# A two-MLP memory attention kernel: the two products of the first MLP are issued under a higher scheduler priority

## The chip, the cores and the metric

The program runs on one core of a Trainium2 chip. The metric is device microseconds of one execution of the whole program. Before the change three runs gave 918.80, 922.19 and 926.05 us; their median is 922.19 us. A measurement of this kernel can tell about one per cent from no change.

The core has four engines that compute, each with an instruction queue that it works off strictly in order: PE (TensorE, matrix products), DVE (VectorE), ACT (ScalarE) and POOL (GpSimd). A fifth, SP, only starts DMA transfers here. An engine that waits at an instruction holds everything behind it in its queue.

## The reference

```python
def _attn_ref(q, k, v, phi):                      # 4 batches, 8 heads, 576 tokens, 64 wide
    a = np.exp(phi - np.max(phi, axis=2, keepdims=True))
    a = a / (np.sum(a, axis=2, keepdims=True) + 1e-09)          # over the tokens, 32 memories
    k_m = np.einsum('bhsm,bhsd->bhmd', a, k)
    v_m = np.einsum('bhsm,bhsd->bhmd', a, v)
    scores = scale * np.matmul(q, k_m.transpose(0, 1, 3, 2))
    attn = np.exp(scores - np.max(scores, axis=-1, keepdims=True))
    attn = attn / (np.sum(attn, axis=-1, keepdims=True) + 1e-09)
    return np.matmul(attn, v_m)
# first MLP: 2304 tokens, 512 -> 2048 -> 512
h = x @ w_in;  g = h / (1 + np.exp(-1.702 * h));  x = g @ w_out
# second MLP: 512 -> 1536 -> 512
xn = x / np.sqrt(np.mean(x * x, axis=-1, keepdims=True) + 1e-06) * rms_g
g = xn @ w_gate;  out = (g / (1 + np.exp(-g)) * (xn @ w_val)) @ w_out
```

q, k, v and phi come as float32. The weights of both MLPs come as float64 and have to be brought to float32 on the chip.

## The kernel before

Every float32 product is made of three passes over rounded parts (high times high, low times high, high times low), so each operand exists as a pair "h" and "l". The four batches are two pairs. attn @ v_m @ w_in is computed as attn @ (v_m @ w_in), so the first MLP starts from v_m @ w_in.

**Attention** is done in units (batch, group of four heads): pair 0 consists of the units (0,0) to (1,1), pair 1 of (2,0) to (3,1). One unit is a chain of small steps that alternate between engines: the maximum over the tokens (PE transposes L229 and L237, DVE, ACT copy L242), the subtraction (POOL L244, 96x768), the exponential (ACT L245 with a table load before it), a sum (DVE L251), the products with k and v (PE L275, tile pk, and the sums L283, tile pk4s), the division by the sums (DVE L287, L290, L291, ACT L297 and L302), transposes (PE L314 to L316), then for q transposes (L338), the scores (PE L360), their softmax (DVE L369 to L384, ACT L374, POOL L385) and the transposes of the result (PE L397, ACT L402).

**The first MLP** runs feature-major over blocks of 256 hidden units: 8 blocks (groups) for each pair, in the order pair 0, groups 0 to 7, then pair 1, groups 0 to 7. Each group has four units t (one half of a batch each). `a_g1` (L442) multiplies the attention with v_m @ w_in on PE (L454, 12 matmuls, tiles pg1 in a PSUM pool of 3), takes the gelu on ACT (L460, tile gf), the rounded part on ACT (L462, tile gr) and the rest on POOL (L109, gr). `a_g2` (L467) multiplies with w_out on PE (L483, 24 matmuls for a unit, tiles pg2 in another PSUM pool of 3) and adds each of four results into x on DVE (L491).

**Weights.** `w_load` lets SP load 128x512 float64 values (three buffers, raw). `w_conv` turns them into float32 on the bits: ACT L152 (absolute value), POOL L153 (clamp), DVE L157, L161 and L164 (shift and merge, tile cv, three buffers); then a DMA on ACT's queue stores the float32 weights for the second pair (L168), POOL L102 rounds them and POOL L109 takes the rest. A group of the first MLP needs four such pieces (two of w_in, two of w_out). On pair 1 the weights are reloaded from that store.

**Order.** The program is written as a list of steps; a scheduler then decides the order of every engine's queue, by priority, along a timeline that it simulates. The first steps are a table written by hand; units 8 to 60 of the first MLP and on (groups 2 to 7 of pair 0, most of pair 1) are written by `run`, a loop that writes for each unit: `a_g1` of this unit, a `w_conv` and a `w_load` of the next group, `vm_next` (v_m @ w_in of the next group, already under `tc.high_priority(100)`), up to two steps of side work (the attention of pair 1, later the RMS norm of pair 0), and `a_g2` of the unit before. Then a second table covers the change to the second MLP, and `run(70, ...)` the rest of it (`b_g3`, `b_g4`). Without an explicit priority, work written earlier is ahead.

Of the kernel before, what the change touches and what calls it, by code (L numbers as in the profile page):

```python
# [18 lines left out]
def kernel(  # L19
# [14 lines left out]
    """Every float32 product is taken as three float32r passes: x = h + l exactly, h being x  # L34
    rounded to float32r, and x*y = h*h' + l*h' + h*l' in float32 accumulation.

    Attention: attn @ v_m @ w_in is taken as attn @ (v_m @ w_in), per batch and head. Two batches
    (a pair) share the array when v_m @ w_in is worked out. The MLPs run feature-major over blocks
    of their hidden units (256 wide), so each weight is loaded and split once per pass; the sums
    over blocks are kept in SBUF.  # L40

    Columns of a pair: batch, parity, chunk pair, p, for token 6 p + 2 (chunk pair) + parity.
    """
# [19 lines left out]
    MINW = 2.0**-15  # bits 0x38000000  # L63
    MAXW = 122872.0  # bits 0x47EFFC00
# [47 lines left out]
    # The first MLP's float32 weights, as they are worked out on the first pass over them.  # L112
    cache = dramp.tile([NA * 4, P, 512], F32, tag="cache", name="cache")
    wt, loaded = {}, {}
# [27 lines left out]
    def w_conv(hf, clamp=G, to_h=G, to_l=G):  # L142
        """float64 to float32, on the bits: sign and top exponent bit, then the other exponent
        bits and the fraction 3 to the left. What is out of float32's range is clamped."""
# [33 lines left out]
    # A unit is four heads of a batch. Where its k and v lay, q^T and the softmax of its scores follow.  # L178
    # The four 32-row blocks of an odd batch hold heads 2, 3, 0, 1.
# [164 lines left out]
    def soft(u, hp):  # L344
        """Of a unit's softmax, blocks 2 hp and 2 hp + 1, by parity and chunk pair; and its sums."""
# [60 lines left out]
    vm = {}  # L406

    def vm_part(pr, g, c):
# [16 lines left out]
        # An odd batch's heads 2, 3, 0, 1 lie in its blocks, so the rows' halves  # L425
        # are of different batches.
# [233 lines left out]
    def vm_next(pr, g, *cs):  # L660
        with tc.high_priority(100):
            for c in cs:
                vm_part(pr, g, c)

    def narrow():
        start_up[0] = False

# [149 lines left out]
```

## Time and profile before

| | before |
|---|---|
| time, median of 3 runs (lowest, highest) | 922.19 us (918.80, 926.05) |
| profiled execution: span from first to last instruction | 919.6 us |
| PE busy, share of the span | 866.3 us, 94% |
| DVE, ACT, POOL busy | 556.7, 382.2, 496.5 us |
| mean granted clock of PE | 0.988 |

The profiled execution's time of its own is given by its span, 919.6 us; it lies inside the range of the three runs and 2.6 us below their median. A row of a timeline has the start in us, the duration, the engine ("ACTq" or "SPq" marks an instruction that only starts a DMA), the line, the operation and the tiles, output before input; in square brackets stands the idle time of the engine just before it and the instruction whose end released it. Buffer numbers are left out of the names in the profile, and pk, pq, pg are shortened names of PSUM tiles.

### The profile page before, as it was taken

The numbers are of one execution on the slowest core, as the hardware profiler recorded it, in microseconds if no ns is written. First come the engines' busy times: TensorE is split into PE (matmuls) and PEld (weight loads), VectorE is DVE, ScalarE is ACT, GpSimd is POOL, SyncE is SP. The second block draws the span as 40 slices with busy tenths as digits, with TensorE's granted clock in tenths as the row PEclk, the third lists the DMA queues.
The fourth block names the chain that finished last, engine by engine and source line by source line (L and its number), as shares of the span: only waits on it lengthen the run. The fifth ranks groups of instructions, "written<-read, shape, count | busy, mean of one in ns | idle before, by whom it ended". The sixth has DMA issues, their size and how long they took to land.

```text
span 919.6 us, 14798 instructions
## 1 busy us (share of the span) xinstructions
PE 866.3 (94%) x5702; PEld 823.1 (90%) x5702; DVE 556.7 (61%) x997; ACT 382.2 (42%) x823; POOL 496.5 (54%) x450
## 2 busy tenths in 40 slices
PE   3887997997999999999998999999999999999997
PEld 2776997986999999999988999999999999999997
DVE  5699896788965456558778155366348328333333
ACT  2366773654667765554466342122122122111110
POOL 2377998897987695979994162064046018001000
PEclk9989998999999999999999999999999999999999
DMA  9974559433221120223313021012004001000123
GB/s 215 258 218 124 165 137 244 160 118 108 90 70 46 48 69 25 69 73 101 92 47 92 1 92 46 1 46 92 0 1 124 14 1 47 1 1 1 46 58 103
DMA packets 40534, 74.62 MB, mean 81 GB/s; under 512 B 3856, under 2 KB 16144, under 8 KB 40464
## 3 DMA queue, kind: packets, MB, share of 16 engines
q1 hardware_dynamic: 35856, 65.29, 26.2%
q10 hardware_dynamic: 4608, 8.39, 2.6%
q8 instruction: 45, 0.74, 0.3%
q14 instruction: 25, 0.20, 0.1%
HBM read 60.56 MB, written 13.11 MB: 80 GB/s over the span
## 4 chain that ended last, share of the span: by engine, by line
PE 72%; POOL 8%; DVE 7%; DMA 6%; issue 4%; SPq 2%; ACT 1%; ACTq 0%; POOLq 0%; DVEq 0%
PE pg L577 31%; PE pg L608 16%; PE pg L483 14%; PE pg L454 7%; POOL cv L153 2%; DMA stage<-in_k_dram 2%; DVE cv L161 2%; PE pvm L422 2%; DMA raw_a_out<-in_moe_w_out_dram 2%; POOL gr L109 2%; DVE cv L164 1%; DVE x L491 1%; DMA stage<-in_v_dram 1%; DVE cv L157 1%; DMA raw_a_in<-in_moe_w_in_dram 1%
## 5 line engine op out<-in xcount | busy, mean ns | idle before, releaser
L483 PE MATMUL pg<-gr,a_outh 128*128 128x288 f32 x1024 | 231.4, 301 | 11.7 <-DVE x L491 10.2
L483 PEld LDWEIGHTS pg<-gr,a_outh 128*128 128x128 f32 x1024 | 172.8, 190 | 16.4 <-DVE x L491 14.7
L483 PE MATMUL pg<-gr,a_outl 128*128 128x288 f32 x512 | 151.6, 297 | 0.0
L153 POOL TENSOR_SCALAR cv<-cv 128x512 f32<-128x512 f32 x67 | 137.1, 2051 | 22.8 <-ACT cv L152 20.8
L608 PE MATMUL pg<-b_o2h,pp 128*128 128x512 f32 x432 | 139.7, 391 | 0.0
L586 DVE TENSOR_TENSOR pf<-sg,pg 128x384 f32<-128x384 f32 x72 | 39.6, 552 | 158.2 <-PE pg L577 151.0
L109 POOL TENSOR_TENSOR gr<-gf,gr 128x288 fp32r<-128x288 f32 x128 | 115.9, 920 | 34.8 <-ACT gr L462 30.1
L491 DVE TENSOR_TENSOR x<-x,pg 128x288 f32<-128x288 f32 x224 | 95.9, 446 | 61.8 <-PE pg L483 60.7
L102 POOL TENSOR_SCALAR b_o2h<-cv 128x512 fp32r<-128x512 f32 x12 | 8.4, 716 | 223.6 <-PE pg L577 223.4
L584 ACT ACTIVATE sg<-pg 128x384 f32<-128x384 f32 x72 | 35.4, 492 | 159.1 <-PE pg L577 159.0
L483 PEld LDWEIGHTS pg<-gr,a_outl 128*128 128x128 f32 x512 | 97.1, 190 | 0.0
L608 PEld LDWEIGHTS pg<-b_o2h,pp 128*128 128x128 f32 x432 | 81.1, 188 | 16.1
L588 ACT CAST pp<-pf 128x384 fp32r<-128x384 f32 x72 | 37.0, 513 | 126.9 <-DVE pf L586 126.6
L608 PE MATMUL pg<-b_o2l,pp 128*128 128x512 f32 x216 | 84.8, 393 | 0.0
L616 DVE TENSOR_TENSOR oacc<-oacc,pg 128x512 f32<-128x512 f32 x90 | 61.1, 683 | 24.1 <-PE pg L608 24.1
L460 ACT ACTIVATE gf<-pg 128x288 f32<-128x288 f32 x128 | 51.6, 410 | 53.4 <-POOL gr L109 25.2
L109 DVE TENSOR_TENSOR pp<-pf,pp 128x384 fp32r<-128x384 f32 x72 | 46.3, 643 | 34.9 <-ACT pp L588 34.9
L462 ACT CAST gr<-gf 128x288 fp32r<-128x288 f32 x128 | 53.5, 432 | 28.8 <-PE pg L483 25.3
L577 PE MATMUL pg<-xnh,b_gateh 128*128 128x384 f32 x288 | 62.6, 337 | 0.0
L577 PE MATMUL pg<-xnh,b_vall 128*128 128x384 f32 x288 | 62.3, 337 | 0.0
L577 PE MATMUL pg<-xnh,b_gatel 128*128 128x384 f32 x288 | 62.3, 336 | 0.0
L157 DVE TENSOR_SCALAR cv<-cv 128x512 uint32<-128x512 uint32 x68 | 52.0, 765 | 17.0 <-POOL cv L153 16.9
(183 smaller groups left out, 1849.4 us busy)
## 6 DMA issues: line engine op xcount, KB each, us to landing
raw_a_in<-in_moe_w_in_dram SPq DMA_DIRECT2D x16, 512.0 KB, 4.2
raw_a_out<-in_moe_w_out_dram SPq DMA_DIRECT2D x16, 512.0 KB, 4.3
cache<-cv ACTq DMA_DIRECT2D x32, 256.0 KB, 3.8
raw_b_gate<-in_moe_w_gate_dram SPq DMA_DIRECT2D x12, 512.0 KB, 3.7
raw_b_val<-in_moe_w_val_dram SPq DMA_DIRECT2D x12, 512.0 KB, 3.8
raw_b_o<-in_moe_w_out_dram SPq DMA_DIRECT2D x12, 512.0 KB, 3.6
stage<-in_k_dram SPq DMA_DIRECT2D x8, 576.0 KB, 12.1
stage<-in_v_dram SPq DMA_DIRECT2D x8, 576.0 KB, 11.6
```

The source lines that it names most:

```text
L109: eng.tensor_tensor(out=lo, in0=full, in1=hi.bitcast(F32), op=ALU.subtract)
L153: clamp.tensor_scalar(out=t.bitcast(F32), in0=t.bitcast(F32), scalar1=MINW, scalar2=MAXW, op0=ALU.max, op1=ALU.min,)
L157: nc.vector.tensor_scalar(out=t, in0=t, scalar1=3, scalar2=0x3FFFFFFF, op0=ALU.logical_shift_left, op1=ALU.bitwise_and,)
L454: nc.tensor.matmul(ps[:, :HALF], lhsT=a[:, b, c, f], rhs=at[:, y, c, n], start=(i == 0), stop=(i == 5),)
L460: nc.scalar.activation(out=gf[:, :HALF], in_=ps[:, :HALF], func=AF.Gelu_apprx_sigmoid)
L462: nc.scalar.copy(out=gr[:, 0, :HALF], in_=gf[:, :HALF])
L483: nc.tensor.matmul(ps[:, :HALF], lhsT=wo[a][:, fc, es], rhs=gr[fc][:, y, :HALF], start=(i == 0), stop=(i == 5),)
L491: nc.vector.tensor_tensor(out=acc[:, e, n], in0=acc[:, e, n], in1=ps[:, :HALF], op=ALU.add)
L577: nc.tensor.matmul(ps[:, :TB], lhsT=w[a][:, e, f], rhs=xs[y][:, e, n], start=(i == 0), stop=(i == 3 * NE - 1),)
L586: nc.vector.tensor_tensor(out=pf, in0=sg, in1=pss[1][:, :TB], op=ALU.mult)
L608: nc.tensor.matmul(ps, lhsT=pp[fc][:, a, ks], rhs=w[y][:, fc], start=(i == 0), stop=(i == 5))
L616: nc.vector.tensor_tensor(out=o, in0=o, in1=ps, op=ALU.add)
```

## The change

A helper `first(n)` opens the scheduler's `high_priority(n)` for n above 0, and does nothing for 0. Inside `run`, the calls of `a_g1` and of `a_g2` are put under `first(150)`; those of `b_g3` and `b_g4` under `first(0)`. The side work, `w_conv` and `w_load` keep their priority, `vm_next` its 100. No instruction is added, removed or altered. Comments and docstrings are dropped too, and the lines of `run` move down by up to five.

```diff
+    def first(n):
+        return tc.high_priority(n) if n else nullcontext()
+
...
         for j, (i, key, t) in list(enumerate(units))[lo:hi]:
             if key == ("a", 1, 0) and t == 1:
                 side, per = norm_side(0), 1
-            (a_g1 if key[0] == "a" else b_g3)(*key[1:], t)
+            with first(150 if key[0] == "a" else 0):
+                (a_g1 if key[0] == "a" else b_g3)(*key[1:], t)
             for hf in at_slot.get(j, []):
                 w_conv(hf)
                 done += 1
...
             for s in islice(side, per):
                 do(s)
-            (a_g2 if prev[0] == "a" else b_g4)(*prev[1:])
+            with first(150 if prev[0] == "a" else 0):
+                (a_g2 if prev[0] == "a" else b_g4)(*prev[1:])
             prev = (*key, t)
```

The effect is on the order of the queues, between the end of the first table (about 112 us into the span) and about 410 us; before and after that stretch PE's order is the same in both kernels. Three places are shown. Numbers behind a tile's name are the program's, the same in both kernels.

ACT's queue in group 4 of pair 0. cache is the store of converted weights, pg_1858 a result of `a_g1`; in brackets are the semaphores that a row waits for, and DMAHW with a number is one of the eight semaphores that the DMAs share. Before:

```order
L152 ACTIVATE cv<-raw_a_4_out_1804 128x512 [waits DMAHW6_49,DMAHW5_49,Pool_49]
L168 DMA cache<-cv 128x512 [waits DMAHW0_49,DVE_49]
L460 ACTIVATE gf<-pg_1769 128x288 [waits PE_49,Pool_49]
L460 ACTIVATE gf<-pg_1781 128x288 [waits PE_49,Pool_49]
L462 CAST gr<-gf 128x288 [waits PE_49,Activation_49]
L242 COPY kmisc_1_1440<-pk_1616 96x128 [waits PE_49]
L168 DMA cache<-cv 128x512 [waits DMAHW2_49,DVE_49]
L462 CAST gr<-gf 128x288 [waits PE_49,Activation_49] x2
L168 DMA cache<-cv 128x512 [waits DMAHW5_49,DVE_49]
L460 ACTIVATE gf<-pg_1858 128x288 [waits Pool_49]
L462 CAST gr<-gf 128x288 [waits PE_49,Activation_49]
L245 ACT_TABLE_LOAD [waits DMAHW7_49]
```

The change:

```order
L152 ACTIVATE cv<-raw_a_4_out_1804 128x512 [waits DMAHW6_49,DMAHW5_49,Pool_49]
L460 ACTIVATE gf<-pg_1769 128x288 [waits PE_49,Pool_49]
L460 ACTIVATE gf<-pg_1781 128x288 [waits PE_49,Pool_49]
L168 DMA cache<-cv 128x512 [waits DMAHW2_49,DVE_49]
L462 CAST gr<-gf 128x288 [waits PE_49,Activation_49] x2
L152 ACTIVATE cv<-raw_a_4_out_1891 128x512 [waits DMAHW3_49,Pool_49]
L168 DMA cache<-cv 128x512 [waits DMAHW4_49,DVE_49]
L462 CAST gr<-gf 128x288 [waits PE_49,Activation_49]
L460 ACTIVATE gf<-pg_1858 128x288 [waits Pool_49]
L242 COPY kmisc_1_1440<-pk_1616 96x128
L460 ACTIVATE gf<-pg_1870 128x288 [waits Pool_49]
L462 CAST gr<-gf 128x288 [waits PE_49,Activation_49] x2
```

Two stores stand between the gelus of pg_1781 and pg_1858 in both. The last of them waited for DMAHW5, which the k load of unit (3,1) uses; now it waits for DMAHW4, which the k load of unit (3,0) uses, three loads earlier on SP's queue, and L152 of raw_a_4_out_1891 stands ahead of it. Four rows behind the fence's end another store waits for DMAHW6 (the q load of unit (3,0)). The load of raw_a_4_out_1891 moves on SP's queue from behind the six loads of the units (3,0) and (3,1) to ahead of them.

DVE's queue in group 6 of pair 0, where the last w_out piece of the group is converted (L157, L161, L164 with raw_a_6_out_2627). Before:

```order
L491 TENSOR_TENSOR x_0_822<-x_0_822,pg_2562 128x288 [waits PE_49]
L491 TENSOR_TENSOR x_0_822<-x_0_822,pg_2570 128x288 [waits PE_49]
L491 TENSOR_TENSOR x_0_822<-x_0_822,pg_2578 128x288 [waits PE_49]
L157 TENSOR_SCALAR cv<-cv 128x512 [waits DMAHW2_49,Pool_49]
L161 SCALAR_TENSOR_TENSOR cv<-raw_a_6_out_2627,cv 128x512 [waits DMAHW3_49,DVE_49]
L164 SCALAR_TENSOR_TENSOR cv<-raw_a_6_out_2627,cv 128x512 [waits DVE_49]
L491 TENSOR_TENSOR x_0_822<-x_0_822,pg_2586 128x288 [waits PE_49]
L491 TENSOR_TENSOR x_0_822<-x_0_822,pg_2643 128x288 [waits PE_49]
L491 TENSOR_TENSOR x_0_822<-x_0_822,pg_2651 128x288 [waits PE_49]
```

The change:

```order
L491 TENSOR_TENSOR x_0_822<-x_0_822,pg_2578 128x288 [waits PE_49]
L384 RECIPROCAL stage_1_1443<-stage_1_1443 96x12 [waits DVE_49]
L491 TENSOR_TENSOR x_0_822<-x_0_822,pg_2586 128x288 [waits PE_49]
L157 TENSOR_SCALAR cv<-cv 128x512 [waits DMAHW2_49,Pool_49]
L161 SCALAR_TENSOR_TENSOR cv<-raw_a_6_out_2627,cv 128x512 [waits DMAHW3_49,DVE_49]
L491 TENSOR_TENSOR x_0_822<-x_0_822,pg_2643 128x288 [waits PE_49]
L164 SCALAR_TENSOR_TENSOR cv<-raw_a_6_out_2627,cv 128x512 [waits DVE_49]
L157 TENSOR_SCALAR cv<-cv 128x512 [waits DMAHW5_49,Pool_49]
L491 TENSOR_TENSOR x_0_822<-x_0_822,pg_2651 128x288 [waits PE_49]
L161 SCALAR_TENSOR_TENSOR cv<-raw_a_7_in_2710,cv 128x512 [waits DMAHW4_49,DVE_49]
L491 TENSOR_TENSOR x_0_822<-x_0_822,pg_2659 128x288 [waits PE_49]
```

The adds L491 stood in one block ahead of the three steps of the conversion and one behind; now one add stands between each two of the steps. On POOL, the subtraction L244 of unit (3,0) stood right behind the clamp of this piece; now it comes in the next group, behind a low part of `a_g1`.

PE's queue at the end of pair 0, where unit (3,1), the last unit of attention, is worked out. pk_3074 is its product with k and v, pk4s its sums, pk_3112 the transposes of the divided result, pq_3189 and pq_3194 transposes of q. Before:

```order
L483 MATMUL pg_3315<-gr,a_6_outl 128x288
L275 MATMUL pk_3074<-stage_1_2826,kmisc_1_2823 32x128 x24
L283 MATMUL pk4s<-ones_f,kmisc_1_2823 128x1
L483 MATMUL pg_3315<-gr,a_6_outh 128x288 x2
L483 MATMUL pg_3315<-gr,a_6_outl 128x288
L483 MATMUL pg_3315<-gr,a_6_outh 128x288
L483 MATMUL pg_3359<-gr,a_7_outh 128x288
L483 MATMUL pg_3359<-gr,a_7_outl 128x288
L483 MATMUL pg_3359<-gr,a_7_outh 128x288 x2
L483 MATMUL pg_3359<-gr,a_7_outl 128x288
L483 MATMUL pg_3359<-gr,a_7_outh 128x288
L483 MATMUL pg_3367<-gr,a_7_outh 128x288
```

The change:

```order
L483 MATMUL pg_3545<-gr,a_7_outh 128x288
L275 MATMUL pk_3074<-stage_1_2826,kmisc_1_2823 32x128 x24
L283 MATMUL pk4s<-ones_f,kmisc_1_2823 128x1
L314 MATMUL pk_3112<-ident,kz 128x128
L315 MATMUL pk_3112<-ident,kz 128x128
L316 MATMUL pk_3112<-ident,vz 128x128
L338 MATMUL pq_3189<-ident,stage_1_2826 128x96 x3
L338 MATMUL pq_3194<-ident,stage_1_2826 128x96 x3
L422 MATMUL pvm<-a_0_inh,vlh_1006 128x256
L454 MATMUL pg_3493<-attnT_536,vm_7h 128x288 x2
L454 MATMUL pg_3493<-attnT_536,vm_7l 128x288 x2
L454 MATMUL pg_3493<-attnT_536,vm_7h 128x288 x2
```

Before, 30 matmuls of L483 and L454 lay between the sums pk4s and the transposes pk_3112 (the fence shows the first half of them). Now pk_3112 follows the sums at once, then pq_3189, and what lay between (the work on pg_3359 to pg_3383) is ahead of pk_2900, the first step of the same unit. From pk_2971 (L237) to the first transposes of the unit's result (L397), PE has 204 matmuls of L483, L454 and L422 in its queue before, and 140 now.

## Rows read from the trace of the kernel before

**Rows 1.** The page, parts 1 and 2: busy time of the engines, and busy tenths in 40 slices of 23 us each.

```profile
PE 866.3 (94%) x5702; PEld 823.1 (90%) x5702; DVE 556.7 (61%) x997; ACT 382.2 (42%) x823; POOL 496.5 (54%) x450
...
PE   3887997997999999999998999999999999999997
...
POOL 2377998897987695979994162064046018001000
PEclk9989998999999999999999999999999999999999
```

**Rows 2.** Busy time by stretch: start and end in us, length, busy time and instructions of PE, PEld, DVE, ACT, POOL, granted clock, DMA share, GB/s.

```profile
120.00:260.00 140.00, 124.43 (x988) 119.27 (x987) 116.85 (x218) 79.71 (x176) 125.45 (x110) 0.96 0.52 145
260.00:310.00 50.00, 50.00 (x435) 49.64 (x435) 25.38 (x56) 36.62 (x83) 38.61 (x43) 1.00 0.20 54
310.00:410.00 100.00, 100.00 (x768) 99.98 (x768) 60.30 (x125) 60.23 (x140) 77.14 (x86) 1.00 0.19 55
```

**Rows 3.** What PE waited for between 120 and 260 us: us in total, times, longest us.

```profile
PE pg L483 <- DVE x L491: 9.5, 8, 5.2
PE pg L454 <- ACT gf L460: 4.0, 1, 4.0
PE pq L397 <- POOL stage L385: 1.1, 1, 1.1
```

**Rows 4.** Timelines of ACT, PE and SP around 157 us.

```profile
156.68 0.33 ACTq L168 DMA_DIRECT2D cache<-cv  x1
157.06 0.41 ACT L460 ACTIVATE gf<-pg 128x288 f32<-128x288 f32 x1 [7.65 <-DMA stage<-in_k_dram]
...
163.52 0.68 ACT L152 ACTIVATE cv<-raw_a_out 128x512 f32<-128x512 f32 x1 [0.48 <-DMA raw_a_out<-in_moe_w_out_dram]
...
153.18 0.29 PE L483 MATMUL pg<-gr,a_outh 128*128 128x288 f32 x1
157.52 0.85 PE L454 MATMUL pg<-attnT,vm_3h 128*128 128x288 f32 x2 [4.04 <-ACT gf L460]
...
136.41 2.39 SPq L209 DMA_DIRECT2D stage<-in_k_dram  x1
```

**Rows 5.** The chain of waits between 130 and 166 us: start, us, what.

```profile
136.41 20.20 DMA stage<-in_k_dram
```

**Rows 6.** Timelines of DVE, POOL and PE around 215 us, and one row of PE at 129 us.

```profile
213.12 0.73 DVE L157 TENSOR_SCALAR cv<-cv 128x512 uint32<-128x512 uint32 x1
213.88 5.53 DVE L161 SCALAR_TENSOR_TENSOR cv<-raw_a_out,cv 128x512 uint32<-128x512 uint32 x1
219.44 1.16 DVE L164 SCALAR_TENSOR_TENSOR cv<-raw_a_out,cv 128x512 uint32<-128x512 uint32 x1
...
213.54 2.02 POOL L244 TENSOR_TENSOR kmisc<-kmisc 96x768 f32<-96x768 f32 x1
215.51 0.79 POOL L109 TENSOR_TENSOR gr<-gf,gr 128x288 fp32r<-128x288 f32 x1
216.28 0.61 POOL L102 TENSOR_SCALAR a_outh<-cv 128x512 fp32r<-128x512 f32 x1
216.86 0.79 POOL L109 TENSOR_TENSOR gr<-gf,gr 128x288 fp32r<-128x288 f32 x1
217.61 1.26 POOL L109 TENSOR_TENSOR a_inl<-cv,a_inh 128x512 fp32r<-128x512 f32 x1
218.82 1.24 POOL L109 TENSOR_TENSOR gr<-gf,gr 128x288 fp32r<-128x288 f32 x1
...
221.03 0.58 PE L483 MATMUL pg<-gr,a_outh 128*128 128x288 f32 x1 [5.25 <-DVE x L491]
...
129.50 0.40 PE L483 MATMUL pg<-gr,a_outh 128*128 128x288 f32 x1 [1.34 <-DVE x L491]
```

**Rows 7.** Busy time by stretch behind the two longest idle times of PE, columns as in rows 2.

```profile
157.50:161.00 3.50, 3.48 (x14) 3.48 (x15) 0.88 (x1) 3.45 (x4) 0.80 (x1) 0.50 1.06 244
161.00:164.00 3.00, 3.00 (x54) 2.44 (x53) 0.98 (x2) 2.45 (x6) 1.65 (x2) 0.66 1.03 384
...
221.00:225.00 4.00, 3.97 (x52) 3.58 (x56) 2.15 (x4) 3.95 (x5) 1.55 (x2) 0.57 0.64 197
```

**Rows 8.** The instructions of L161 between 120 and 260 us: ns min/median/max, first and last start.

```profile
L161 DVE SCALAR_TENSOR_TENSOR cv<-raw_a_out,cv x10: 675/706/5527, 123.4 to 250.5; 128x512 uint32<-128x512 uint32 x10
```

**Rows 9.** Timelines of PE, ACT and DVE between 261 and 295 us, rows of unit (3,1) alone.

```profile
261.94 0.27 PE L237 MATMUL pk<-ident,mx 128*96 128x128 f32 x1
...
265.67 0.85 ACT L245 ACTIVATE kmisc<-kmisc 96x768 f32<-96x768 f32 x1
...
268.37 0.54 PE L275 MATMUL pk<-stage,kmisc 96*32 96x128 f32 x12
...
269.82 0.38 PE L283 MATMUL pk4s<-ones_f,kmisc 96*128 96x1 f32 x2
...
270.63 0.97 DVE L291 TENSOR_SCALAR rv<-maskeo,rv 128x3 f32<-128x3 f32 x1
...
272.58 0.31 ACT L297 ACTIVATE kz<-pk,rv 128x64 f32<-128x64 f32 x1
...
274.10 0.27 PE L314 MATMUL pk<-ident,kz 128*128 128x128 f32 x1
...
294.20 0.49 PE L397 MATMUL pq<-ident,stage 96*128 96x96 f32 x4
```

**Rows 10.** Busy time by stretch at the same place, columns as in rows 2.

```profile
262.20:268.37 6.17, 6.17 (x49) 6.01 (x47) 3.18 (x5) 5.52 (x9) 4.83 (x6) 1.00 0.16 41
...
262.20:294.20 32.00, 32.00 (x295) 31.64 (x294) 19.32 (x44) 22.48 (x48) 23.51 (x27) 1.00 0.15 42
```

More of the change, by code (lines that the diff above doesn't have):

```diff
@@ L1 @@
-from contextlib import ExitStack
+from contextlib import ExitStack, nullcontext
 from itertools import islice
```

## The prediction

> **What bounds the kernel now.** I read the page first: PE is busy 94% of the span, so only its idle time and its slow clock can be won, and both lie before 260 us and once near 485 us [rows 1]. The table by stretch says it in numbers: from 260 to 410 us PE is busy 150.0 of 150.0 us at clock 1.00, and from 120 to 260 us it lacks 15.6 of 140 us at clock 0.96 [rows 2]. In the first of these two, a new order can only lose; in the second it can win. From 410 us PE's order is the same in both kernels, so I carry whatever is won or lost by then to the end unchanged.
>
> What PE waits for between 120 and 260 us is almost all the MLP's own evacuations, not weights and not PE: 9.5 us for the adds L491 in eight waits, one of them 5.2, and one wait of 4.0 us for the gelu L460 [rows 3]. Both long ones are side work ahead of the MLP in a queue:
>
> - At 157 us ACT sits 7.65 us in front of a gelu. The instruction ahead of it is a store of converted weights, which starts at 156.68; the chain of waits shows why: it waits for a k load of attention, issued at 136.41 and landed 20.20 us later, at 156.61 [rows 4, 5]. The store has nothing to do with that load but the semaphore. PE is idle 4.04 us for it [rows 4].
> - At 213.88 a step of the weight conversion, L161, takes 5.53 us on DVE, where its median is 0.71 [rows 6, 8]. During it POOL runs L244 and five more instructions without a gap [rows 6]. One add stands behind L161 and L164 on DVE, and PE is idle 5.25 us [rows 6].
>
> **What the change does, part by part.** No instruction is added or removed; what moves is the order of PE, ACT, DVE, POOL and SP. The sum is made against the profiled execution, 919.6 us; the median of the runs is 2.6 us higher.
>
> *The store at 157 us.* In the new order the store ahead of this gelu waits for the k load of unit (3,0), three loads earlier, while the w_out load, moved ahead, comes in front. From 156.61 the v and q loads of (3,1) and the w_out load land by 163.52 [rows 4, 5], so a load takes about 6.9 / 3 = 2.3 us. The k load of (3,0) then lands near 156.6 − 3 × 2.3 + 2.3 = 152.0, and the next store's load, q of (3,0), near 156.6. PE had work until 153.5 [rows 4], so the gelu at 152 is in time. Gone is the idle 4.0 us. Gone too is the slow clock behind it: 3.5 us at 0.50 (the lower of its two levels, 1.2 of 2.4 GHz) and 3.0 us at 0.66 [rows 7], which is 3.5 × 0.50 + 3.0 × 0.34 = 2.8 us. Together −6.8 us. The least is 0 (another store, another load), and that is an end of the range.
>
> *The conversion at 214 us.* L244 moves away from this L161 and an add comes between any two steps. Whether the next L161 meets POOL's dense stretch again is not to be read from an order, so I bound it: at best idle and clock go, 5.25 + 4.0 × 0.43 = 7.0 us [rows 6, 7]; at worst nothing. I take −5.7 us: a shorter wait for an add stays in its place, 1.3 us as at 129.50 [rows 6] (the other seven are 0.6 on average, (9.5 − 5.2) / 7 [rows 3]), and the clock stays up. The trace has L161 held for 5.53 us, over six POOL instructions [rows 6]. The Trainium skill (SBUF — State Buffer, "Who interferes with whom") says that a DVE instruction with two inputs in SBUF contends with a GpSimd instruction that reads SBUF, and that whoever has the shared pair keeps it for the whole instruction, the other being blocked. By that rule L161 would wait for L244 alone, until 215.56, and take 2.4 us; the trace disagrees with it in the length. By the rule this term would be −7.0 and the forecast 917.8, since no meeting with POOL could then hold the adds for long. By the row it is −5.7, and the row speaks against the change: low parts put ahead on POOL make such a stretch without a gap likelier.
>
> *The remaining small waits* before 260 us, 15.6 − 4.0 − 5.25 = 6.3 us [rows 2, 4, 6], I leave as they are: the adds go ahead of side work now (bound −3), but PE also gets to the next group's weights earlier, and POOL, which makes them, is busy 125.5 of 140 us [rows 2] with no priority for `w_conv`. For that I add +1 us (0 to +4).
>
> *The end of pair 0, 262 to 294 us.* This is where the displaced work falls due. Unit (3,1)'s chain runs from L237 at 261.94 to L397 at 294.20, 32.3 us, and PE is fully busy meanwhile [rows 9, 10]. In the new order PE has 64 large matmuls fewer in between (140 against 204). One costs 6.17 / 49 = 0.126 us [rows 10], so 8.1 us of cover go. Walking the chain with the new queue:
>
> 1. From L237 to the end of the exponential took 266.52 − 261.94 = 4.6 us [rows 9]; the cover is 24 matmuls, 3.1 us. Idle 1.5.
> 2. The sums end at 270.20 and the transposes L314 follow at once. Ahead of them must come the division: L291 ends at 271.60, one ACT step of 0.31 follows, so 271.95 at the earliest, 274.10 as it was [rows 9]. Idle 1.8 to 3.9; I take 2.2, since ACT is less crowded there.
> 3. The rest (the first v_m @ w_in product waits for the unit's last copies, the scores for q's transposes, L397 for the softmax) has the other 116 of the 140 matmuls and small products as cover. I put it at 1.0 for each of the three, 3.0 together, by the wait of 1.1 us for L385 [rows 3].
>
> That is 6.7 us, between 3 (ACT and DVE free at once) and 8.1 (the chain as long as before). An idle time of 5.25 us lowered the clock by 1.7 us worth [rows 6, 7]; I add it once: +8.4 us. The upper end, 8.1 and two such clock losses, is +11.5; the lower is +3.
>
> *The rest of the stretch to 410 us* (side work moved among itself, the RMS norm of pair 0): PE is saturated there [rows 2], and I cost it at nothing. Its cover is that full PE; if an L385 came late there, it would cost 1 us as in the wait for L385 [rows 3].
>
> **Sum:** −6.8 − 5.7 + 1.0 + 8.4 = −3.1 us against the profiled execution, 916.5. On the scale of the median, 922.2 − 3.1 = **919.1 us**.
>
> **Rivals.**
>
> - *Nearly all early idle time goes and the boundary is covered* (faster). For it: both long waits are the MLP behind side work, just what a priority reorders [rows 3]. Against: the sums followed at once by the transposes that need them cannot be covered. It gives −6.8 − 7.0 − 3 + 3 = −13.8: about 908. Chance 0.22, with what lies between it and my forecast.
> - *The boundary costs it all and the early stalls only move* (slower). The place is PE's queue from L237 to L397 of unit (3,1): with the attention put behind the MLP in every queue, its links wait also on ACT and POOL for gelus and low parts, so the chain stays at 32.3 us or grows with 8.1 us less on PE. It decides when the early gain is below the boundary's loss by 9 us. With +11.5 there, +1, and no early gain, 922.2 + 12.5 = 934.7. For it: POOL has no time to spare in groups 3 to 7 [rows 1, 2], so a stall of 5 us can be formed anew. Against: the first stall's reason is a plain queue order that is gone. Chance 0.22.
> - *It does nothing that shows*: what is won before 260 us is paid back at 262 to 294, as in my sum, or the order changes among waits of the same size. 913.0 to 931.4; its likeliest part is 914 to 927. Chance 0.56, my forecast within it.
>
> **How the numbers follow.** About one per cent is what a measurement of this kernel can tell from no change: below 913.0 is faster, above 931.4 slower. The likeliest is the sum, 919.1, with its own range 914 to 927 (early gain −6.8 to −13.8, boundary +3 to +11.5, not all at their ends). To hold 8 in 10 I go to the fast rival, 907, and up to 934, short of the slow rival's end. Faster 0.22, same 0.56, slower 0.22.
>
> **What the changed profile would show.** For the store: no idle time on ACT with a stage load as its releaser near 150 us, and no clock below 0.9 between 150 and 165. For the conversion: no L161 above 3 us in front of an add for which PE waits over 2 us. For the boundary: PE idle 5 to 9 us between about 245 and 285 us, released by ACT L245 and L297 and by POOL L385, with a granted clock below 1.00 behind it. For the end: from 410 us on the same intervals as before, the idle time of 3 us near 485 among them. The forecast is wrong if PE's idle time at the boundary is under 3 us, if a new wait over 3 us stands in groups 3 to 6, or if the stretch behind 410 us changes in length by over 2 us.

## The result: slower, 935.6 us

| | before, in the same comparison | the change |
|---|---|---|
| median (lowest to highest) | 920.5 us (917.5 to 926.1) | 935.6 us (934.3 to 936.8) |
| ratio, 95% interval | | 1.0149 [1.0112, 1.0186] |
| span of the profiled execution | 919.6 us | 933.8 us |

The forecast of 919.1 us and its range to 934 are missed; the time is near that of the slow rival, 934.7 us. In a second comparison the changed kernel took 931.0 us, 1.0094 [1.0064, 1.0124], so the loss is 0.9 to 1.5%, and two comparisons of one kernel can differ by half a per cent. Executions that lasted 1691 us or more are left out of the ratios, and the profiled one of h2_late_unit (2152.64 us) is among them, so that this run has a time and no rows.

The page of the changed kernel, the lines that answer to [rows 1]:

```profile
PE 871.5 (93%) x5702; PEld 824.8 (88%) x5702; DVE 563.1 (60%) x997; ACT 381.5 (41%) x823; POOL 496.5 (53%) x450
...
PE   3787988998998899999998999999999999999998
...
POOL 2377999799846686889986073045027008001000
PEclk9969999999998999999998999999999999999999
```

Busy time by stretch, as in [rows 2]:

```profile
120.00:260.00 140.00, 127.15 (x995) 120.64 (x994) 118.13 (x210) 73.96 (x169) 128.60 (x113) 0.98 0.52 148
260.00:310.00 50.00, 43.54 (x362) 41.91 (x362) 26.11 (x60) 32.11 (x67) 26.70 (x29) 0.93 0.11 32
310.00:410.00 100.00, 97.16 (x737) 95.91 (x736) 56.14 (x113) 62.39 (x143) 76.82 (x84) 1.00 0.18 54
```

From 120 to 260 us PE gained 2.7 us of busy time. From 260 to 410 us, where it had been busy without a gap, it lost 6.5 and 2.8 us, and in the first of the two stretches its clock fell to 0.93. The order of PE's matmuls is the same again not from 410 us, as I had read it, but from 430.9 us before and 444.2 in the change. From there on the two kernels run nearly alike: PE's wait for L528 near the end of the first MLP is 3.36 us before and 3.37 now, and it comes 13.4 us later (485.60 and 498.97). Around it the clock is 0.50 for longer in the change (498.1 to 504.9 us, against 487.3 to 490.7 before), and at the end the change is 14.2 us late. PE's rows before and in the change:

```profile
485.60 0.52 PE L535 MATMUL pnr<-ident,r 128*128 128x128 f32 x3 [3.36 <-DVE r L528]
```

```profile
498.97 0.87 PE L535 MATMUL pnr<-ident,r 128*128 128x128 f32 x3 [3.37 <-DVE r L528]
```

**The early part.** The stall of ACT at 157 us is gone. ACT's timeline of the changed kernel has the store at 152.19 and the gelu 0.8 us behind it, and no row there waits for a load of attention:

```profile
146.65 0.37 ACTq L168 DMA_DIRECT2D cache<-cv  x1
...
152.19 0.37 ACTq L168 DMA_DIRECT2D cache<-cv  x1
152.66 0.43 ACT L462 CAST gr<-gf 128x288 fp32r<-128x288 f32 x1 [2.29 <-DVE x L491]
153.00 0.41 ACT L460 ACTIVATE gf<-pg 128x288 f32<-128x288 f32 x1
```

The L161 of 5.53 us at 214 us is gone too, but in this execution another L161 met a like stretch of POOL, which begins with an L244 and has no gap. Timelines of DVE, POOL and PE, changed kernel:

```profile
157.85 4.21 DVE L161 SCALAR_TENSOR_TENSOR cv<-raw_a_out,cv 128x512 uint32<-128x512 uint32 x1
161.99 0.44 DVE L491 TENSOR_TENSOR x<-x,pg 128x288 f32<-128x288 f32 x1
...
157.50 2.02 POOL L244 TENSOR_TENSOR kmisc<-kmisc 96x768 f32<-96x768 f32 x1
159.48 0.81 POOL L109 TENSOR_TENSOR gr<-gf,gr 128x288 fp32r<-128x288 f32 x1
160.25 1.27 POOL L109 TENSOR_TENSOR a_outl<-cv,a_outh 128x512 fp32r<-128x512 f32 x1
161.47 1.25 POOL L109 TENSOR_TENSOR gr<-gf,gr 128x288 fp32r<-128x288 f32 x1
...
162.48 0.40 PE L483 MATMUL pg<-gr,a_outh 128*128 128x288 f32 x1 [1.85 <-DVE x L491]
```

Between 120 and 260 us PE now has 13 waits, the longest of 1.85 us; before it had 11, with the two long ones. What PE waited for there, as in [rows 3], the three largest:

```profile
PE pg L483 <- DVE x L491: 8.7, 8, 1.8
PE pg L454 <- DVE vm_3l L109: 1.3, 1, 1.3
PE pvm L422 <- ACT gf L460: 1.1, 1, 1.1
```

**The end of pair 0.** The same view between 260 and 412 us, where [rows 2] had no wait at all:

```profile
PE pg L454 <- ACT gf L460: 3.0, 4, 1.1
PE pk L314 <- ACT kz L297: 2.6, 1, 2.6
PE pg L483 <- ACT x L106: 2.3, 1, 2.3
PE pq L338 <- ACT stage L106: 0.5, 1, 0.5
```

The wait of 2.6 us is the link that follows the sums at once. The chain of waits of the changed kernel there (start, us, what):

```profile
277.86 1.40 DVE kmisc L251
...
279.31 0.40 PE pk4s L283 x2
...
279.73 0.68 DVE vm_0l L109
...
280.43 0.77 DVE vm_0l L109 x2
...
281.21 0.17 DVE rv L287
...
281.92 0.32 ACT kz L297
...
282.29 0.33 PE pk L314
```

Three DVE instructions of `vm_next` stand ahead of the division and take 1.45 us of it. The wait of 2.3 us comes later, in pair 1. ACT's and PE's timelines of the changed kernel:

```profile
301.21 1.28 ACT L374 ACT_TABLE_LOAD   x1
302.50 0.52 ACT L374 ACTIVATE stage<-stage 96x384 f32<-96x384 f32 x1
302.93 0.50 ACT L512 CAST sr<-sq 128x384 fp32r<-128x384 f32 x1
303.34 1.22 ACT L433 CAST vm_1h<-pvm 64x512 fp32r<-64x512 f32 x3
304.58 0.70 ACT L106 COPY x<-pg 128x288 f32<-128x288 f32 x2
...
305.04 0.40 PE L483 MATMUL pg<-gr,a_outh 128*128 128x288 f32 x1 [2.25 <-ACT x L106]
```

ACT is still at the softmax of unit (3,1), with a table load, while PE already needs ACT's copies of pair 1's first results. Before, the same L397 came at 294.20 [rows 9]; here it comes at 308.30.

The waits for gelus have one thing in common. When ACT changes from an exponential or from the RMS norm (L525) back to the gelu, it loads a table, 1.28 us here. ACT and PE of the changed kernel:

```profile
311.79 1.28 ACT L460 ACT_TABLE_LOAD   x1
313.08 0.71 ACT L460 ACTIVATE gf<-pg 128x288 f32<-128x288 f32 x2
...
313.54 0.54 PE L454 MATMUL pg<-attnT,vm_0h 128*128 128x288 f32 x2 [1.11 <-ACT gf L460]
```

The other waits for a gelu in this stretch stand 1.8 us behind the start of such a load as well (loads at 297.76, 316.02, 355.61 and 393.00). Before, the same stretch has five such loads (266.54 to 381.48), and PE, busy all the time, waits behind none of them.

### The profile page after: what moved, and what is told of

Its sections match the earlier page's. It is cut to its first block, busy times and chain, and to the rows that moved or that the text cites. A ratio compares the mean times of both kernels' runs of the same rounds, so it can differ in the third digit from the quotient of the medians.

```text
span 933.8 us, 14790 instructions
## 1 busy us (share of the span) xinstructions
PE 871.5 (93%) x5702; PEld 824.8 (88%) x5702; DVE 563.1 (60%) x997; ACT 381.5 (41%) x823; POOL 496.5 (53%) x450
## 4 chain that ended last, share of the span: by engine, by line
PE 68%; POOL 9%; DVE 8%; issue 5%; ACT 4%; DMA 4%; SPq 2%; ACTq 0%; POOLq 0%; DVEq 0%
PE pg L577 30%; PE pg L608 15%; PE pg L483 12%; PE pg L454 7%; POOL gr L109 3%; POOL cv L153 2%; DVE cv L161 2%; DMA raw_a_out<-in_moe_w_out_dram 2%; PE pvm L422 1%; DVE cv L164 1%; DMA stage<-in_v_dram 1%; DVE cv L157 1%; DVE x L491 1%; POOL a_inl L109 1%; POOL a_outl L109 1%
## 5 line engine op out<-in xcount | busy, mean ns | idle before, releaser
L483 PE MATMUL pg<-gr,a_outh 128*128 128x288 f32 x1024 | 231.5, 301 | 13.1 <-DVE x L491 9.8
L483 PEld LDWEIGHTS pg<-gr,a_outh 128*128 128x128 f32 x1024 | 173.1, 190 | 17.9 <-DVE x L491 13.3
L483 PE MATMUL pg<-gr,a_outl 128*128 128x288 f32 x512 | 151.2, 297 | 0.0
L491 DVE TENSOR_TENSOR x<-x,pg 128x288 f32<-128x288 f32 x224 | 96.2, 447 | 54.2 <-PE pg L483 53.3
L102 POOL TENSOR_SCALAR b_o2h<-cv 128x512 fp32r<-128x512 f32 x12 | 8.4, 715 | 224.9 <-PE pg L577 224.7
L483 PEld LDWEIGHTS pg<-gr,a_outl 128*128 128x128 f32 x512 | 97.3, 190 | 0.0
L608 PEld LDWEIGHTS pg<-b_o2h,pp 128*128 128x128 f32 x432 | 81.1, 188 | 16.1
L157 DVE TENSOR_SCALAR cv<-cv 128x512 uint32<-128x512 uint32 x68 | 55.0, 809 | 20.0 <-POOL cv L153 19.8
L577 PE MATMUL pg<-xnh,b_valh 128*128 128x384 f32 x288 | 62.4, 337 | 0.0
```

What stands on the lines that cost most here:

```text
L157: nc.vector.tensor_scalar(out=t, in0=t, scalar1=3, scalar2=0x3FFFFFFF, op0=ALU.logical_shift_left, op1=ALU.bitwise_and,)
L483: nc.tensor.matmul(ps[:, :HALF], lhsT=wo[a][:, fc, es], rhs=gr[fc][:, y, :HALF], start=(i == 0), stop=(i == 5),)
L491: nc.vector.tensor_tensor(out=acc[:, e, n], in0=acc[:, e, n], in1=ps[:, :HALF], op=ALU.add)
L577: nc.tensor.matmul(ps[:, :TB], lhsT=w[a][:, e, f], rhs=xs[y][:, e, n], start=(i == 0), stop=(i == 3 * NE - 1),)
L608: nc.tensor.matmul(ps, lhsT=pp[fc][:, a, ks], rhs=w[y][:, fc], start=(i == 0), stop=(i == 5))
```

## The experiments

I give for each run the place of the last attention unit in PE's queue: how many large matmuls (L454, L483, L422) stand ahead of its last transposes, L397 of unit (3,1). It is 1296 before and 1334 in the change. For profiled executions I sum PE's idle time and its slow clock ((1 − granted clock) × busy time) over windows of 2 us, for 112 to 260 us and for 260 to 412 us. All ratios are to the kernel before in the same comparison. Group numbers are those of pair 0; units with j below 24 are groups 2 to 5.

### Where the priority stands

```diff
-            with first(150 if key[0] == "a" else 0):
+            with first(150 if j < 24 else 0):
...
-            with first(150 if prev[0] == "a" else 0):
+            with first(150 if j < 24 else 0):
```

**e1_early.** 

> The priority of 150 ends with group 5 of pair 0; groups 6 and 7 and all of pair 1 have none, as in the kernel before. PE's order is that of the change up to group 5, and in it the first step of the last attention unit, L237 of unit (3,1), stands behind 1200 large matmuls (L454, L483, L422), against 1092 before and 1194 in the change; between that step and L397 lie 126 of them, against 204 and 140. Theory 1 (the loss is made early, by putting the attention behind the MLP, and only falls due at the end of pair 0): as slow as the change, 930 to 936 us against 920.5. Theory 2 (the loss is made by the order of group 7 and of pair 1 itself, where the MLP goes ahead of the unit's steps): the gain of groups 2 to 5 alone, 915 to 919 us.

Measured: 935.0 us, 1.0117 [1.0070, 1.0163]. Its profiled execution took 927.2 us, the other three 934.3 to 935.8, so its rows show less than its time.

```diff
-            with first(150 if key[0] == "a" else 0):
+            with first(150 if j >= 24 and key[0] == "a" else 0):
...
-            with first(150 if prev[0] == "a" else 0):
+            with first(150 if j >= 24 and prev[0] == "a" else 0):
```

**e2_late.** 

> The opposite: no priority up to group 5 of pair 0, 150 from group 6 on and in pair 1. L237 of unit (3,1) stands behind 1110 large matmuls, with 221 of them up to L397. Theory 1: like the kernel before, 919 to 924 us. Theory 2: like the change, 930 to 936 us.

Measured: 938.2 us, 1.0167 [1.0139, 1.0194].

```diff
-            with first(150 if prev[0] == "a" else 0):
+            with first(0):
```

**e4_g1.** 

> Only a_g1 has the priority of 150, a_g2 none. L237 of unit (3,1) stands behind 1073 large matmuls, with 172 of them up to L397: 32 less cover than before, 4 us at 0.126 us each, and they fall only on the places where PE has nothing else. Theory 1: 918 to 924 us. Theory 2 (the raised MLP itself): between the kernels, 924 to 932 us.

Measured: 1.0015 [0.9998, 1.0031], 923.5 us.

```diff
-            for s in islice(side, per):
-                do(s)
+            with first(150 if j < 36 else 0):
+                for s in islice(side, per):
+                    do(s)
```

**e9_side.** 

> As the change, and the attention of pair 1 has the same 150 in groups 2 to 7 of pair 0 and at the start of pair 1, so that only the weight conversion and loads stay behind. L237 of unit (3,1) stands behind 1110 large matmuls, with 216 up to L397. Theory 1: the loss at the end of pair 0 is gone, PE idle under 2 us between 260 and 330 us, and the time is 915 to 921 us. Theory 3 (the weights, put behind everything, are what is late): 930 us or more, with PE or ACT waiting for L164, L102 or raw loads.

Measured: 932.3 us, 1.0106 [1.0073, 1.0138].

Theories 1, 2 and 3 fall. The early half and the late half each cost as much as the whole, and e2_late and e9_side have 221 and 216 large matmuls between L237 and L397, more than the 204 of before, and still lose. Theory 3's time came in e9_side, but not its waits: between 112 and 412 us PE waits nowhere for L164, L102 or a raw load, and ACT once, 0.7 us, for a raw load. What the four slow kernels share is a late L397 (1326 to 1334); the fast one has an early one (1245). This suggests theory 4, which the next runs test: PE has by then worked off what doesn't need the unit, and the unit's end, with the gelus, exponentials and copies that ACT owes at the start of pair 1, lies bare.

### The place of the last unit, alone

Three runs start from the kernel before, with nothing of the MLP raised (both `first` get 0), and lower the side steps of unit (3,1) by 150, 100 and 120:

```diff
             for s in islice(side, per):
-                do(s)
+                with first(-150 if s[0].__name__.startswith("att") and (3, 1) in s else 0):
+                    do(s)
```

**h2_late_unit.** 

> The kernel before, without any priority of the MLP; only the side steps of unit (3,1) are lowered by 150. PE's order up to that unit is that of before, and its last transposes, L397, stand behind 1346 large matmuls (L454, L483, L422) instead of 1296; the change has 1334 there, and the three slow kernels run so far 1326 to 1331, the fast ones 1296 and 1245. Theory 4 (what costs is that the end of the last attention unit comes when PE has worked off nearly every matmul that does not need it, whatever put it there): as slow as the change, 930 to 938 us. Theory 5 (what costs is a_g2 put at once behind a_g1, so that PE waits for each gelu and cast): like before, 919 to 925 us.

Measured: 935.6 us (935.1 to 937.6), 1.0160 [1.0135, 1.0184].

**k100_late_unit.** 

> The kernel before with the side steps of unit (3,1) lowered by 100 instead of 150, nothing else. In PE's order L397 of that unit then stands behind 1292 large matmuls, near the 1296 of before, so that 42 of the 1334 that do not need the unit are left for its end. Theory 4: like before, 919 to 924 us. If lowering the unit's steps costs by itself, on ACT or DVE: 926 us or more.

Measured: 922.9 us, 1.0006 [0.9982, 1.0029].

**k120_late_unit.** 

> The same, lowered by 120: L397 stands behind 1346 large matmuls, L237, L275 and L314 stay behind 1092, 1142 and 1176 (1092, 1140 and 1170 before). Theory 4: 930 to 938 us, with 8 us or more of idle time and slow clock of PE between 260 and 412 us (none before, 12.5 in the change), released by ACT L460, L374's line or copies of ACT. If the place of L397 is not what counts: 919 to 925 us.

Measured: 931.5 us, 1.0100 [1.0067, 1.0134]. What PE waited for between 260 and 412 us, first k100, then k120:

```profile
PE pg L454 <- ACT gf L460: 0.4, 1, 0.4
```

```profile
PE pg L454 <- ACT gf L460: 3.8, 3, 1.8
PE pg L454 <- ACT attnT L402: 1.3, 1, 1.3
```

This is the experiment that carries the verdict. Nothing is raised, PE's order up to the unit is that of before, and the two kernels differ by 20 in one offset: with L397 behind 1292 matmuls it costs nothing, behind 1346 it costs 1%. So a late last unit is enough for a loss of this size. (That L397 can stand behind 1346 also shows that more than the 1334 of the expectations don't need the unit.) Of the 8 us expected between 260 and 412 us only 5.1 show as idle time, but the time is there: from PE's 1795th matmul to its 3111th, the same two and the same work between them in all three kernels, it takes 166.1 us before, 167.1 with 100 and 174.3 with 120. The waits agree with those of the changed kernel in part. The three for gelus stand behind a table load, as there; the one for attnT does not occur there, and the change's waits for kz and for copies into x, 4.9 us, do not occur here. The longest, 1.84 us at 349.08, comes 47 us behind L397 and behind the RMS norm's table loads; how the unit's place brings that one about is not shown.

### One product alone

```diff
-            with first(150 if key[0] == "a" else 0):
+            with first(0):
```

**e5_g2** (a_g2 raised, a_g1 not). 

> Only a_g2 has the priority of 150, a_g1 none. L397 of unit (3,1) stands behind 1331 large matmuls. Theories 4 and 5 both: as slow as the change, 930 to 938 us. If it is like before, neither holds and it takes both products together.

Measured: 926.2 us, 1.0060 [1.0038, 1.0083], slower than before, but less than both theories had. The end costs as expected, 10.4 us between 260 and 412 us, but the early part gains 10.7 (9.1 us of loss against 19.8).

```diff
-            with first(150 if key[0] == "a" else 0):
+            with first(150 if j >= 32 and key[0] == "a" else 0):
...
-            with first(150 if prev[0] == "a" else 0):
+            with first(150 if j >= 32 and prev[0] == "a" else 0):
```

**e8_pair1** (both raised in pair 1 alone). 

> The priority of 150 for both products in pair 1 alone, none in pair 0. L397 of unit (3,1) stands behind 1304 large matmuls, 8 more than before, while a_g2 goes ahead of the RMS norm and the rest of the side work in pair 1. Theory 4: like before, 919 to 925 us. Theory 5: slower, 928 us or more, with PE idle for L460 and L106 between 285 and 400 us.

Measured: 929.5 us, 1.0085 [1.0057, 1.0112]; between 260 and 412 us it loses 4.1 us, one wait of 1.96 us for a gelu and the slow clock behind it among them. The time is theory 5's, and L397 is near its old place: a raised MLP in pair 1 does cost something of its own. ACT and PE show what:

```profile
286.81 1.28 ACT L374 ACT_TABLE_LOAD   x1
...
289.10 1.28 ACT L460 ACT_TABLE_LOAD   x1
...
291.29 1.28 ACT L374 ACT_TABLE_LOAD   x1
...
293.12 1.28 ACT L460 ACT_TABLE_LOAD   x1
...
294.88 0.40 PE L454 MATMUL pg<-attnT,vm_0h 128*128 128x288 f32 x1 [1.96 <-ACT gf L460]
```

A gelu stands between the two exponentials (L374) of unit (3,1) and brings two more table loads, and PE waits for the gelu behind the last. Before, one load (283.52) serves both exponentials. The change has the same split, with loads of L374 at 295.60 and 301.21. How much of its loss is due to that is not separated; e1_early, with nothing raised in pair 1 and no split, loses as much without it.

```diff
-            with first(150 if prev[0] == "a" else 0):
+            with first(0):
...
-    run(8, 61, ("a", 0, 1, 3), side, 2)
+    run(8, 61, ("a", 0, 1, 3), side, 3)
```

**g1_g1per3** (a_g1 raised; the loop takes three side steps). 

> Only a_g1 has the priority of 150, and the loop writes three side steps for each unit where it wrote two. L397 of unit (3,1) stands behind 1243 large matmuls, so that 91 are left for its end. Theory 4: no loss at the end of pair 0, PE idle under 2 us between 260 and 330 us, and not slower than before: 916 to 923 us. Theory 5: the same, as a_g2 is not raised.

Measured: 923.1 us, 1.0011 [0.9991, 1.0030]; 1.6 us lost at the end of pair 0, as expected.

### Raised early, with the unit in its place

Of i5_g2_16; i8_g2_20_p3 has `j < 20` there, and 3 side steps as in g1_g1per3:

```diff
-            with first(150 if key[0] == "a" else 0):
+            with first(0):
...
-            with first(150 if prev[0] == "a" else 0):
+            with first(150 if j < 16 else 0):
```

**i5_g2_16.** 

> Only a_g2 has the priority of 150, and only in groups 2 and 3 of pair 0. L397 of unit (3,1) stands behind 1296 large matmuls, as before. Theory 4: nothing lost at the end of pair 0; of the early gain (10.7 us between 112 and 260 us with a_g2 raised alone all through) the part of these groups, about half: 914 to 921 us. If a raised a_g2 costs by itself: 924 us or more.

Measured: 917.6 us, 0.9945 [0.9927, 0.9963]. This version beats both kernels, by little: the gain over before is as large as the difference between the two comparisons of the changed kernel. Busy time by stretch:

```profile
112.00:260.00 148.00, 137.00 (x1100) 132.05 (x1099) 120.54 (x234) 87.23 (x192) 140.17 (x122) 0.98 0.49 140
260.00:412.00 152.00, 152.00 (x1215) 151.57 (x1214) 88.80 (x186) 97.30 (x224) 117.36 (x127) 1.00 0.20 58
```

**i8_g2_20_p3.** 

> Only a_g2 has the priority of 150, in groups 2 to 4 of pair 0, and the loop writes three side steps for each unit where it wrote two, so that the attention is written earlier. L397 stands behind 1296 large matmuls. Theory 4: nothing lost at the end of pair 0 and most of the early gain of 10.7 us kept: 911 to 918 us. If a raised a_g2 costs by itself: 924 us or more.

Measured: 921.3 us, 0.9980 [0.9965, 0.9995], above the 911 to 918 expected: nothing lost at the end, but less gained early. A raised a_g2 does not cost by itself here.

### How little is enough

The edits are those of e1_early with `j < 16` and `j < 12`, of e1_early's first line alone with `j < 16` (the second `first` gets 0), and none.

**l1_both16** (both, groups 2 and 3). 

> Both products have the priority of 150, but only in groups 2 and 3 of pair 0. L397 of unit (3,1) stands behind 1331 large matmuls, so 3 of the 1334 are left for its end. Theory 4: slower than before by the loss at the end of pair 0 (8 to 12 us) less the early gain: 925 to 935 us. If the priority must stand near the end of pair 0 to cost anything: 915 to 921 us.

Measured: 935.2 us, 1.0148 [1.0112, 1.0185].

**l3_both12** (both, group 2 alone). 

> Both products have the priority of 150 in group 2 of pair 0 alone, four units of 61. L397 of unit (3,1) stands behind 1331 large matmuls. Theory 4: 925 to 935 us, with 8 us or more of idle time and slow clock between 260 and 412 us. If so short a stretch can't cost: 919 to 923 us.

Measured: 934.4 us, 1.0128 [1.0099, 1.0158].

**l2_g1_16** (a_g1 alone, groups 2 and 3). 

> Only a_g1 has the priority of 150, in groups 2 and 3 of pair 0. L397 of unit (3,1) stands behind 1296 large matmuls, as before and as in the run with a_g2 alone in these groups (917.6 us against 922.8). Theory 4: nothing lost at the end of pair 0. If raising a_g1 removes the early waits as a_g2 does: 915 to 919 us; if the early gain is a_g2's: 920 to 924 us.

Measured: 920.5 us, 0.9986 [0.9967, 1.0006]: nothing lost at the end, no gain beyond the interval.

**after_again.** 

> The changed kernel once more, for a second profile. If its small early gain (3.7 us of idle time and slow clock less than before, between 112 and 260 us) is the kernel's own: idle time there 12 to 13.5 us and slow clock 2 to 4 us again. If it was that execution's: slow clock under 1 us there, as in the run whose priority ends with group 5 and whose order up to there is the same.

Measured: 931.0 us, 1.0094 [1.0064, 1.0124]; between 112 and 260 us 11.3 us idle and no slow clock. Neither expectation fits whole. The slow clock was the first execution's, and so was 1.5 us of the idle time: the wait of 1.85 us behind the L161 of 4.21 us has no match here. The 11.3 us agree with e1_early, whose order up to there is the same (11.5).

| run | ratio | matmuls ahead of L397 | lost 112 to 260 us (idle + slow clock) | lost 260 to 412 us |
|---|---|---|---|---|
| before | 1 | 1296 | 15.6 + 4.2 | 0 |
| g1_g1per3 | 1.0011 | 1243 | 13.2 + 3.2 | 1.6 |
| e4_g1 | 1.0015 | 1245 | 13.7 + 1.5 | 2.4 |
| k100_late_unit | 1.0006 | 1292 | 13.7 + 6.2 | 0.5 |
| i5_g2_16 | 0.9945 | 1296 | 11.0 + 2.8 | 0 |
| i8_g2_20_p3 | 0.9980 | 1296 | 14.4 + 1.6 | 0 |
| l2_g1_16 | 0.9986 | 1296 | 13.8 + 4.4 | 0 |
| e8_pair1 | 1.0085 | 1304 | 14.5 + 5.0 | 4.1 |
| e1_early | 1.0117 | 1326 | 11.5 + 0 | 11.5 |
| e9_side | 1.0106 | 1326 | 14.7 + 1.7 | 8.0 |
| e2_late | 1.0167 | 1331 | 15.7 + 3.9 | 8.9 |
| e5_g2 | 1.0060 | 1331 | 9.1 + 0 | 10.4 |
| l1_both16 | 1.0148 | 1331 | 12.5 + 1.5 | 10.4 |
| l3_both12 | 1.0128 | 1331 | 14.4 + 6.2 | 7.7 |
| the change | 1.0149 | 1334 | 12.8 + 3.3 | 12.5 |
| after_again | 1.0094 | 1334 | 11.3 + 0 | 13.9 |
| k120_late_unit | 1.0100 | 1346 | 14.7 + 4.5 | 5.1 |

Up to 1296 at most 2.4 us are lost at the end of pair 0, at 1304 4.1, and from 1326 on 5 to 14 us. Within that last group the loss does not rise with the place: the latest, k120_late_unit, shows the least.

## Why the prediction was wrong

- **The store at 157 us, −6.8 us:** right in mechanism, the wait is gone. The slow clock behind it did not go with it: in the profiled execution it was 0.66 from 154 to 158 us, after other waits. In the second execution there was none.
- **The conversion at 214 us, −5.7 us:** the L161 there is short now, at most 1.19 us from 213 us on; but the race with POOL came up again, twice: L161 took 4.21 us at 157.85, and L164, the step behind it, 2.81 us at 221.21. PE waited 1.85 and 1.52 us for the adds behind them, 3.4 where I had left 1.3. The second execution has the L164 alone. I had bounded this from an order that can't tell it.
- **The remaining small waits, +1.0 us:** with both stalls gone, 15.6 − 4.0 − 5.25 + 1.3 + 1.0 = 8.6 us of idle time should have been left; 12.8 were (11.3 the second time). Without the waits behind L161 and L164 that is about +3 us for this term, inside its 0 to +4.
- **The early part as a whole** was −11.5 us; it measured −3.7 (19.8 to 16.1), and −8.5 in the second execution. Two steps failed here: that the clock stays up once the stalls are gone (3.3 us of slow clock in the first execution, none in the second), and the size of the waits that are left (4.2 us too many, 2.7 the second time). Raising a_g2 alone gave −10.7, near the forecast; why both together give less was not settled.
- **The end of pair 0, +8.4 us:** the place was right and the size not far off: up to L397 at 308.30 PE is idle for 6.5 us and loses 3.2 to the clock, 9.7 together and within 3 to 11.5. The links were not right. Link 1 cost 0.4 (the wait for L251) for 1.5, link 2 cost 2.6 for 2.2, and of the 3.0 for three more links only 0.5 shows (L338). The other 2.9 us are waits of pair 1's first products for a gelu (0.6) and a copy of ACT (2.25), which stand ahead of L397 in PE's queue. My walk did not have them, since it followed the links of the unit alone.
- **The measure was wrong as well.** I counted the 64 matmuls that went from between L237 and L397. e2_late and e9_side have more there than before and lose 8.9 and 8.0 us. What goes with the loss is how late L397 stands in the whole queue; k100_late_unit and k120_late_unit show it alone, and e8_pair1 shows that it is not the only thing that can cost.
- **The rest to 410 us at nothing:** this is the step that failed behind the end of pair 0. I had taken PE's full busy time there as cover that would stay. Behind L397 PE is idle for another 2.8 us in four waits for gelus, 1.3 of it from 330 to 412 us. With the 2.9 us above, 5.7 of the 9.3 us of idle time are waits of pair 1's own products for ACT. The end and the rest together measured 9.3 + 3.2 = 12.5 us for 8.4.
- **The slow rival** gave 934.7 us by the full loss at the end and no early gain. The loss is confirmed, and so is its mechanism: the chain from L237 to L397 grew from 32.3 us to 34.4 (273.93 to 308.30), with 64 matmuls fewer in it. That the early stalls only move was true by half. That its number lies so near the measured one is in part luck: it left out an early gain of 3.7 us, and also 4.6 us of waits that idle time does not show.
- **The three signs of being wrong** that I had named did not come: PE's idle time from 245 to 285 us is 5.0 us, no wait in groups 3 to 6 is above 1.85 us, and the stretch behind the common order is 1.0 us longer. They looked for one long wait, and the loss is in many short ones. What did differ from the picture I gave is the clock, 0.66 from 154 to 158 us.

Idle time and slow clock together rise by 8.8 us from 112 to 412 us (−3.7 + 12.5), and the kernel is 13.4 us late by 499 us. The difference of 4.6 us is nearly all in waits that the view hides: a matmul's row lasts 0.29 us while matmuls start 0.13 us apart, so each wait takes 0.16 us more than its idle time. There are 23 waits of 0.4 us or more in PE's timeline behind 100 us, against 10 before, which makes 2 us. Most of the other 2.6 us is in matmuls that start late without any idle time in front of them: from the first matmul of group 2 to where the order is the same again, 125 start more than 0.05 us later than is usual behind their predecessor, against 105 before, by 12.3 us against 9.6 in all. So of the 16.5 us between the −3.1 of the sum and the 13.4, 7.8 are early gain that did not come, 4.1 the end of pair 0 and the rest, and 4.6 waits that the sum had no term for.

## What to carry to other kernels

Side work that a later stage needs is not free work to be put off: the main work beside it is its cover, and a priority for the main work uses that cover up, early and without a wait that shows, until the last link of the side chain stands bare. Find that last link in the queue and count how much independent work is left behind it, before and after; here raising the four units of one group was enough to move it. Then look at what the main work itself needs from the engine that the chain ends on: here PE waited 5.7 us for ACT's gelus and copies and 3.6 us for the chain's own links. Raise only the product whose waits the profile shows, only where they are, and see that the last link stays in its place: that gave 0.55% in one comparison, where raising both all through cost 0.9 to 1.5%.

## What the hardware showed that I had not expected

- A VectorE instruction with two inputs in SBUF can be held over several GpSimd instructions that follow each other without a gap. L161, at least 0.68 us long, took 5.53 us from 0.34 us behind the start of an L244 before [rows 6], over five GpSimd instructions and into a sixth, and 4.21 us from 0.35 us behind one in the change, over three and into a fourth. L164, in the change at 221.21, took 2.81 us in the same way, over three and into a fourth. That GpSimd holds them is read from the rows; no run here takes its instructions away. In the second execution of the changed kernel the same L161 came at 155.17, 1.6 us ahead of that L244, and took 0.98 us. The Trainium skill (SBUF — State Buffer, "Who interferes with whom") has the one that comes second blocked for the other's whole instruction; by that rule L161 would have ended near 159.52 + 0.68 = 160.2, an estimate, behind L244 alone, and the trace has 162.06: it agrees that it is blocked, not for how long.
- The same queue and much the same waits do not give the same clock. PE's last two waits ahead of this stretch are 0.42 and 1.17 us in the first execution and 0.41 and 1.16 in the second, and the second has no slow clock at all between 112 and 260 us. Busy time by stretch of the changed kernel, first and second execution:

```profile
154.00:158.00 4.00, 4.00 (x24) 4.00 (x23) 1.99 (x5) 0.18 (x1) 3.84 (x5) 0.66 1.09 287
```

```profile
154.00:158.00 4.00, 4.00 (x33) 4.00 (x32) 3.35 (x7) 2.11 (x6) 3.92 (x4) 1.00 1.08 285
```

- The start-up, in which PE's order is the same in all these kernels, took between 111.1 us (e1_early) and 116.4 us (e8_pair1) up to the first matmul of group 2, with 0 to 9.0 us of slow clock between 40 and 112 us. A single profile can't tell differences below that; the repeated times and the stretch behind it can.
